# A second path through a transformer block: where its code lies, and how the kernel ends

## The chip, the core and the metric

The kernel runs on one core of a Trainium2 chip. The metric is the device time of one execution in microseconds (us), reported as the median of several runs. Each of the core's engines (TensorE or PE, VectorE or DVE, ScalarE or ACT, GpSimd or POOL, SyncE or SP) has its own stream of instructions; semaphores order them against each other. A branch is taken by each engine for itself.

## The reference

One block of a transformer in pre-norm form, sequence 2048, width 640, in bf16: attention with 32 query heads of 20 columns that share one key and one value head, then a gated feed-forward layer of width 1536.

```python
def _A_ref(x, wq, wk, wv, wo):
    q = heads(x @ wq); k = x @ wk; v = x @ wv
    scores = jnp.einsum("bhqd,bkd->bhqk", q, k) * (Dh ** -0.5)
    p = _softmax(scores, axis=-1)
    ...
    return o @ wo

def _B_ref(x, w_gate, w_up, w_down):
    h = _gelu(x @ w_gate) * (x @ w_up)
    return h @ w_down

h  = x + _A_ref(_layernorm(x), ...)
h2 = h + _B_ref(_layernorm(h), ...)
```

## The kernel before

**Two paths.** The main path computes the softmax without subtracting row maxima: it exponentiates the scores as they are, sums them with the values (a column of ones in `v_ext` gives the sum), and divides. That is right as long as the sums are neither too small nor too large. So the kernel checks the reciprocals of all sums (`rL`) against two bounds, brings the outcome into one integer (`flag`), and every engine loads it into a register (`good`). If all is well, each engine branches to the block `all_done`; otherwise it falls into the block `with_maximum`, which computes everything again with row maxima. With the inputs of the reference the second path is not run, but its code lies between the branch and `all_done` in each engine's stream.

**The planner.** Every piece of work is a task (`sc.add`) with its engine, an estimated duration, dependencies, a priority and the buffers it takes and gives back. `_Sched.schedule` runs them in simulation and writes down one order for each engine (`order`), `resolve` works out the semaphore waits, `emit` writes the instructions. `HOT` is a large negative priority (first come), `hold` lets a task reserve its engine for a moment. Nothing is reordered at run time.

**The work.** Sixteen tiles of 128 rows. The scores of a tile go through PSUM in groups of two or three banks to ScalarE's exponential (L978, tile `pbuf`); some go to VectorE instead (L932, L943, tile `dbuf`). TensorE multiplies the result with `v_ext`. Between them TensorE does the projections and the feed-forward matmuls of earlier tiles (L534), whose results VectorE adds to the rows in `xh` (L1276). SP issues all transfers and DMA transposes after the start.

**The last tile** (`last_tile`) has no other attention work to hide behind, and is laid out for a short chain: transposed sums and their reciprocal (L1111, L1113), normalised output (L1118), transposes and copy (L1139, L1142), the output projection into two PSUM banks (L1308, tasks `wa`, `wb`), statistics of the layer norm (L1322) and copies to `xh` by ACT (L1324, task `bx`), normalisation (L1328 to L1334, the power on POOL, L1331), transposes (L1348) and copies by ACT and DVE (L1355, tasks `bte`), the residual into the accumulators (L1301, task `again`), gate and up matmuls (L1372), GELU (L1399), product (L1404), down matmuls (L1381), eviction of the two halves (L1415, tasks `fin`) and their output (L1417). ACT's table for the GELU is loaded right behind the last exponential (L1339).

**The end of the main path.** `raise_flag` is called after `last_tile`. The checks of all sums but the last pass come early; those of the last pass are held back behind the layer norm of the last tile (`state["last_nm"]`): three small DVE operations (L1157, L1159, L1161), a product (L1168), a matmul with a constant that spreads the outcome over the partitions (L1171, task `okm`), a conversion to an integer (L1173), the register load on each engine (L1178) and, right behind it, a branch hint on each engine (L1179): an instruction that names the target of a later branch ahead of time. `run` wraps each path in a block (`nc.Block`, L1498), which ends with a barrier of all engines. Then comes the branch (L1527), and in `all_done` SP waits until all outputs have landed (the wait's record has line L1520).

Of the kernel before, what the change touches and what calls it, by code (L numbers as in the profile page):

```python
# [45 lines left out]
class _Sched:  # L46
# [363 lines left out]
    def emit(self, eng_name, eng, sems):  # L410
        for t in self.order[eng_name]:
            for s, v in self.waits.get(t, ()):
                eng.wait_ge(sems[s], v)
            ins = t.fn(eng)
            if t.sem is not None:
                ins.then_inc(sems[t.sem], 16 if t.dma is not None else 1)


def bass_sequential_preLN__grouped_kv_mqa__glu_gated_geglu__prompt_kernel(
# [308 lines left out]
    q_ready, q_evicted, q_slot = {}, {}, {}  # L728
    all_qk = {}
# [21 lines left out]
    def q_dma(t, tk, g0=0):  # L751
        tr = sc.add("sp", lambda e: e.dma_start_transpose(
            qT[:, q_slot[t].index, g0:NG, :], q_tok[:, tk.index, 4 * g0:H, :].rearrange("p a b -> p (a b)")),
# [14 lines left out]
    def q_first(tk):  # L768
# [23 lines left out]
        for j, eng in ((0, "act"), (1, "dve")):  # L792
# [12 lines left out]
            def ev(e, j=j, eng=eng, view=view):  # L805
                o = qT[:, q_slot[0].index, 2 * j:2 * j + 2, :]
# [68 lines left out]
    def qk_mm(e, bk, item):  # L875
        t, h, kt, hl = item
        r = slice(32 * hl, 32 * hl + 32)
        return e.matmul(bk.rearrange("p (g n) -> p g n", g=4), kT4[r, kt * P:(kt + 1) * P],  # L878
                        qT[r, q_slot[t].index, 4 * h:4 * h + 4, :], start=True, stop=True, tile_position=(32 * hl, 0))
# [285 lines left out]
    def raise_flag():  # L1165
        early = check_sums(0, 2 * NT - 1, 0, 0.45)
        late = check_sums(2 * NT - 1, 2 * NT, 1, 0.14, [state["last_nm"]])
        c = sc.add("dve", lambda e: e.tensor_tensor(okay_b[:], okay_all[:, 0:1], okay_all[:, 1:2], ALU.mult), 0.2,  # L1168
                   [early, late], prio=HOT + 2, name="okb")
        ax, bk = aux()  # L1170
        m = sc.add("pe", lambda e: e.matmul(bk()[:, 0:1], halves[:, 0:P], okay_b[:], start=True, stop=True), 0.1,  # L1171
                   [c, t_halves], prio=HOT / 4, acq=[ax], name="okm")
        f = sc.add("dve", lambda e: e.tensor_scalar(flag[:], bk()[:, 0:1], 2.0, None, ALU.mult), 0.2, [m], prio=HOT / 4,  # L1173
                   rel=[ax], name="flag")

        for eng in sc.ENGINES:
            def fn(e, eng=eng):
                ins = e.reg_load(good[e.engine], flag[0:1, 0:1])  # L1178
                hints[e.engine] = e.mark_branch_hint_location()  # L1179
                return ins  # L1180
            sc.add(eng, fn, 0.6, [f], prio=1e6, after=late_on.get(eng, []), name=f"good_{eng}")

    late_on = {}
# [99 lines left out]
    def last_tile(t, ont):  # L1283
# [37 lines left out]
        for j, c0, c1 in halves_:  # L1321
# [17 lines left out]
        tab = sc.add("act", lambda e: e.activation(warm[:], warm[:], ACT.Gelu_apprx_tanh), 2.7, state["exps"], prio=1e7,  # L1339
                     name="gelu_table")  # L1340
        lnT = []
# [17 lines left out]
        late_on["act"], late_on["dve"] = lnT[:1], lnT[1:]  # L1359
# [52 lines left out]
        downs(2)  # L1412
        for j, c0, c1 in halves_:
            fin = add("dve" if j else "act", lambda e, j=j, c0=c0, c1=c1: (
                e.tensor_copy(xh[:, t, c0:c1], acc(j)) if j else e.activation(xh[:, t, c0:c1], acc(j), ACT.Copy)), 0.45,  # L1415
                [dn[j], nm], rel=[a_sl], name=f"fin{j}_{t}")
            outs.append(sc.add("sp", lambda e, c0=c0, c1=c1: e.dma_start(out_view[:, t, c0:c1], xh[:, t, c0:c1]), 2.0,  # L1417
                               [fin], prio=nprio(), dma="d_out", name=f"out{j}_{t}"))

# [57 lines left out]
    raise_flag()  # L1477
# [11 lines left out]
    sem_cms = []  # L1489

    def run(plan, wait_out):
# [6 lines left out]
        with nc.Block() as block:  # L1498

            @block.sync  # L1500
            def _(e):
                wait_out(e)
                plan.emit("sp", e, sems)

            @block.scalar
            def _(e):
                plan.emit("act", e, sems)

            @block.tensor
            def _(e):  # L1510
                plan.emit("pe", e, sems)

            @block.vector
            def _(e):
                plan.emit("dve", e, sems)

            @block.gpsimd
            def _(e):
                plan.emit("pool", e, sems)
        return lambda e: e.wait_ge(sems["d_out"], plan.totals["d_out"])  # L1520

    out_done = run(sc, lambda e: None)


    for e in nc.engines.values():
        if e.engine in hints:
            e.br_eq(good, P, on_true="all_done", on_false="with_maximum").branch_hint(hints[e.engine])  # L1527
    with nc.body("with_maximum"):
        sc = _Sched()
        SA_pool, PV_pool, AUX_pool = _Pool(1), _Pool(1), _Pool(2)  # L1530
        LN_pool, XN_pool, ON_pool, ONT_pool, HH_pool, G_pool = (_Pool(4), _Pool(NXB), _Pool(1), _Pool(2), _Pool(2),
                                                                _Pool(2))
        OTK_pool, QTK_pool, QT_pool = _Pool(2), _Pool(2), _Pool(1)
        PR_pool, PT_pool, MX_pool = _Pool(NPB), _Pool(2), _Pool(2)
        t_half = t_ident = dma_wg = dma_wu = dma_wd = None
        z_q, tail, q_evicted, state["qk"] = [], [None, "d_oT"], {}, None
        dma_wq = [None, None]
        wo_ready, outs = [], []
        last_in = None

        def head(t, g, hl, q_done, q_sl, heads):

            r = slice(32 * hl, 32 * hl + 32)
            s_sl, p_sl, t_sl, m_sl = SA_pool.slot(), PR_pool.slot(), PT_pool.slot(), MX_pool.slot()
# [95 lines left out]
```

## Time and profile before

| | |
|---|---|
| time, median of 3 runs | 761.51 us (759.73 to 764.65) |
| profiled execution: time | 761.73 us |
| profiled execution: span, first to last instruction | 760.0 us |
| PE busy | 720.2 us (95%) |
| ACT busy | 728.3 us (96%) |
| DVE busy | 675.8 us (89%) |
| POOL busy | 190.3 us (25%) |
| mean granted TensorE clock | 0.990 |

The span counts from the first to the last instruction record of any engine, branches and semaphore waits included, while "busy" leaves those out. The execution's time is 1.7 us longer than its span. In the rows of the profile, "PEld" is TensorE's weight load, "SPq", "PEldq" and the like are an engine's queue instructions (loads of registers, branches, waits), "L1178" is line 1178 of the kernel before. A row of a line's records reads: engine, operation, count, shortest/median/longest duration in ns, start of the first and the last. The window rows read: window, its length, busy time and count of PE, PEld, DVE, ACT and POOL, the granted clock, the share of the DMA engines, GB/s.

### The profile page before, as it was taken

How to read it: one execution, taken by the hardware profiler on the slowest of the kernel's cores; microseconds unless marked ns; L12 is line 12 of the kernel's file. 1: busy time of each engine (PE TensorE's matmuls, PEld its weight loads, DVE VectorE, ACT ScalarE, POOL GpSimd, SP SyncE). 2: the span in 40 equal slices, each digit the busy share in tenths (PEclk: the TensorE clock that was granted, in tenths of full speed). 3: DMA queues.
4: the chain of work that ended last, by engine and by line, in shares of the span. 5: the costliest groups of instructions: out<-in, count | busy, mean ns of one | idle time of the engine just before them, and what ended most of it. 6: DMA issues, size and time to landing. Idle time of an engine off the chain costs nothing.

```text
span 760.0 us, 23793 instructions
## 1 busy us (share of the span) xinstructions
PE 720.2 (95%) x10601; PEld 262.3 (35%) x10601; DVE 675.8 (89%) x1271; ACT 728.3 (96%) x701; POOL 190.3 (25%) x257
## 2 busy tenths in 40 slices
PE   7889889999999999999999999999999999999996
PEld 3332223333333333333333333333333332323335
DVE  8679999997998899999998988998999999898872
ACT  6899999999999999999999999999999999999981
POOL 6310001151335134103304133140321012251500
PEclk9699999999999999999999999999999999999999
DMA  6893011020111102120100202012021200110020
GB/s 172 135 343 73 1 26 17 2 45 19 24 31 41 33 2 46 20 45 19 31 16 19 45 20 46 19 16 45 5 46 31 41 11 10 40 22 20 14 52 22
DMA packets 80623, 31.68 MB, mean 42 GB/s; under 512 B 71552, under 2 KB 79232, under 8 KB 80512
## 3 DMA queue, kind: packets, MB, share of 16 engines
q1 hardware_dynamic: 79200, 30.03, 18.4%
q8 instruction: 84, 1.38, 0.8%
q10 hardware_dynamic: 1312, 0.05, 0.1%
q14 instruction: 27, 0.22, 0.1%
HBM read 10.21 MB, written 2.62 MB: 17 GB/s over the span
## 4 chain that ended last, share of the span: by engine, by line
ACT 61%; PE 28%; DVE 7%; DMA 2%; POOL 1%; issue 0%
ACT pbuf L978 60%; PE ps L534 10%; PE ps L878 9%; PE ps L1092 7%; DVE dbuf L932 2%; ACT g_z L1257 1%; DMA xnT<-xn_tmp 1%; PE ps L1372 1%; DVE dbuf L943 1%; DMA onT<-oN 1%; POOL g_z L1217 0%; DVE g_us L1251 0%; PE ps L1381 0%; DVE xn_tmp L649 0%; DVE stats L626 0%
## 5 line engine op out<-in xcount | busy, mean ns | idle before, releaser
L978 ACT ACTIVATE pbuf<-ps 128x1024 bf16<-128x1024 f32 (+1 forms) x661 | 700.8, 1226 | 6.1 <-PE ps L878 5.4
L932 DVE TENSOR_SCALAR dbuf<-ps 128x512 int16<-128x512 f32 x520 | 341.5, 681 | 35.9 <-PE ps L878 33.2
L878 PE MATMUL ps<-qT,kT 32*128 32x512 bf16 x2048 | 289.0, 387 | 17.1 <-ACT pbuf L978 12.0
L943 DVE TENSOR_SCALAR dbuf<-dbuf 128x2048 int16<-128x2048 int16 x260 | 172.8, 690 | 0.7
L878 PEld LDWEIGHTS ps<-qT,kT 32*128 32x128 bf16 x2048 | 76.2, 91 | 255.4 <-ACT pbuf L978 191.5
L1092 PE MATMUL ps<-pbuf,v_ext 128*32 128x512 bf16 (+3 forms) x2032 | 146.1, 334 | 1.7 <-ACT pbuf L978 1.5
L1092 PE MATMUL ps<-dbuf,v_w 128*32 128x512 bf16 x1560 | 133.9, 382 | 4.3 <-DVE dbuf L932 1.7
L1245 POOL TENSOR_TENSOR g_z<-g_gs 128x512 bf16<-128x512 bf16 x45 | 48.7, 1082 | 131.2 <-DVE g_gs L1243 131.2
L1092 PEld LDWEIGHTS ps<-pbuf,v_ext 128*32 128x32 bf16 x2032 | 44.4, 94 | 71.3 <-issue 51.1
L534 PE MATMUL ps<-wg_sb,xnT 128*32 128x512 bf16 x900 | 67.9, 383 | 0.7 <-DVE dbuf L932 0.2
L534 PE MATMUL ps<-wd_sb,hhT 128*32 128x320 bf16 x1440 | 67.6, 301 | 0.5 <-DMA hhT<-g_us 0.2
L534 PE MATMUL ps<-wu_sb,xnT 128*32 128x512 bf16 x900 | 67.3, 382 | 0.5
L1118 POOL TENSOR_TENSOR oN<-oT,rL 128x320 bf16<-128x320 f32 x30 | 22.2, 739 | 160.0 <-DVE rL L1113 159.7
L1092 PEld LDWEIGHTS ps<-dbuf,v_w 128*32 128x32 bf16 x1560 | 38.5, 95 | 40.7 <-DVE dbuf L943 12.5
L632 POOL CAST lnvb<-mv 128x1 bf16<-128x1 f32 x31 | 7.3, 236 | 171.5 <-DVE mv L630 170.8
L1217 POOL TENSOR_TENSOR g_z<-g_z,g_gs 128x512 bf16<-128x512 bf16 x36 | 41.1, 1168 | 30.5 <-DVE g_z L1254 30.5
L1217 POOL TENSOR_TENSOR g_us<-g_z,g_us 128x512 bf16<-128x512 bf16 x36 | 40.6, 1155 | 24.7 <-DVE g_z L1260 24.7
L534 PEld LDWEIGHTS ps<-wd_sb,hhT 128*32 128x32 bf16 x1440 | 31.9, 96 | 26.6 <-issue 15.8
L1251 DVE SCALAR_TENSOR_TENSOR g_us<-ps,g_gs 128x512 bf16<-128x512 f32 x45 | 30.6, 681 | 4.9 <-PE ps L534 4.7
L534 PE MATMUL ps<-wq_sb,xnT 128*32 128x320 bf16 (+1 forms) x660 | 31.7, 298 | 1.1 <-DVE xnT L682 0.4
L1243 DVE CAST g_gs<-ps 128x512 bf16<-128x512 f32 x45 | 30.4, 676 | 1.7 <-PE ps L534 1.5
L534 PE MATMUL ps<-wo_sb,onT 128*32 128x320 bf16 x600 | 30.5, 302 | 1.3 <-DVE dbuf L932 0.8
(98 smaller groups left out, 363.5 us busy)
## 6 DMA issues: line engine op xcount, KB each, us to landing
out_dram<-xh SPq DMA_DIRECT2D x15, 160.0 KB, 1.8
wg_sb<-in_B_w_gate_dram SPq DMA_DIRECT2D x1, 1920.0 KB, 10.6
wu_sb<-in_B_w_up_dram SPq DMA_DIRECT2D x1, 1920.0 KB, 15.0
wd_sb<-in_B_w_down_dram SPq DMA_DIRECT2D x1, 1920.0 KB, 19.7
xh<-in_A_x_dram SPq DMA_DIRECT2D x2, 640.0 KB, 7.1
xh<-in_A_x_dram SPq DMA_DIRECT2D x3, 320.0 KB, 3.8
wq_sb<-in_A_wq_dram SPq DMA_DIRECT2D x2, 400.0 KB, 4.9
wo_sb<-in_A_wo_dram SPq DMA_DIRECT2D x1, 800.0 KB, 4.9
```

The lines of the kernel that those rows point to most:

```text
L534: ins = e.matmul(out[r, :], lhs[:, r], rhs, start=start, stop=stop, tile_position=(0, 32 * b))
L878: return e.matmul(bk.rearrange("p (g n) -> p g n", g=4), kT4[r, kt * P:(kt + 1) * P], qT[r, q_slot[t].index, 4 * h:4 * h + 4, :], start=Tr ...
L932: quad["bits"].append(sc.add("dve", lambda e: e.tensor_scalar(part(seg, w=slice(512 * item[0], 512 * item[0] + 512)), bk(), D_BIAS, 0.0, A ...
L943: dep = [sc.add("dve", lambda e, j=j, s=s: e.tensor_scalar(part(s), part(seg), D_SHIFT[j], None, ALU.add), 0.602, bits, prio=0.55 * HOT + ...
L978: exps.append(sc.add("act", lambda e, w0=w0, w1=w1, to=to: e.activation(pbuf[:, to:to + w1 - w0], ps[:, w0:w1], ACT.Exp, scale=EXP_SCALE), ...
L1092: ins = e.matmul(ps[32 * b:32 * b + 32, PVB * 512 + a:PVB * 512 + a + n].rearrange("p (a n) -> p a n", n=32), x[2], span.rearrange("p (a n ...
L1118: onorm[(t, h)] = c = sc.add(by, lambda e: e.tensor_tensor(oN[:, otk.index, h * (D // 2):(h + 1) * (D // 2)].rearrange("p (g l d) -> p l g ...
L1217: return [sc.add("pool", lambda e, c=slice(512 * j, 512 * j + 512): e.tensor_tensor(out[:, k.index, c], a[:, k.index, c], b[:, k.index, c] ...
L1243: ge = sc.add("dve", lambda e, col=col, bk=bk: e.tensor_copy(g_gs[:, gsl.index, col], bk()), d_ps(512), [gm], prio=EVAC + pr, rel=[ax], na ...
L1245: sqt = sc.add("pool", lambda e, col=col: e.tensor_tensor(g_z[:, gsl.index, col], g_gs[:, gsl.index, col], g_gs[:, gsl.index, col], ALU.mult),
L1251: uts.append(sc.add("dve", lambda e, col=col, bk=bk: e.scalar_tensor_tensor(g_us[:, gsl.index, col], bk(), 0.5, g_gs[:, gsl.index, col], A ...
L1257: th = sc.add("act", lambda e: e.activation(g_z[:, gsl.index, :], g_z[:, gsl.index, :], ACT.Tanh, scale=GELU_C), d_act(1536), zt, prio=-5. ...
```

## The change

It moves code, and with it the jumps over it, and it moves the checks.

- **Place of the second path's code.** For SP, POOL and ACT it now lies in the middle of the main path, in a block `with_maximum_1`; they jump over it there without condition (SP and POOL where the planner's order has their widest gap, ACT behind the last exponential). In the order that results, SP jumps behind the transpose of the queries that follows the first tile's output transpose, POOL behind its last product `g_z` of the feed-forward layer. At the end these three fall through to `all_done` when the flag is good and go back to `with_maximum_1` when it is not. For PE and DVE the second path (`with_maximum_2`) stays at the end, and they branch over it.
- **No block, no barrier.** The orders are emitted straight into the program; the barrier between the two paths is replaced by waits at the head of the second path.
- **Checks.** The checks of the last pass no longer wait for the layer norm. In DVE's order two stand before the copy of L1142, the minimum and the product behind it, the integer flag behind L1330. The matmul `okm` stands behind L1308 on PE and uses the bank of the attention sums. The register loads stand at the end of each stream on SP, ACT and PE (behind its last down matmuls), on DVE before the three products of L1404.
- **Hint.** Only PE has one, right behind L1308 (task `wb`), ahead of 36 of the matmuls of L534 that lay before L1301; four of the 40 now lie behind it.
- **Last eviction.** Both halves of the last output are evicted by ACT.
- **GELU table.** Its load stands behind ACT's copies of L1324.

```diff
 def raise_flag():
     early = check_sums(0, 2 * NT - 1, 0, 0.45)
-    late = check_sums(2 * NT - 1, 2 * NT, 1, 0.14, [state["last_nm"]])
+    late = check_sums(2 * NT - 1, 2 * NT, 1, 0.14)
...
-    ax, bk = aux()
+    ax, bk = pvb()
...
-            ins = e.reg_load(good[e.engine], flag[0:1, 0:1])
-            hints[e.engine] = e.mark_branch_hint_location()
...
+def flag_loads(f):
+    late_on.update(act=[ends[-1]], pe=[ends[0]], sp=outs[-1:])
+    for eng in sc.ENGINES:
+        sc.add(eng, lambda e: e.reg_load(good[e.engine], flag[0:1, 0:1]), 0.55, [f],
+               prio=1e6 if eng != "dve" else HOT, after=late_on.get(eng, []), name=f"good_{eng}")
...
 # last_tile
-    tab = sc.add("act", lambda e: e.activation(warm[:], warm[:], ACT.Gelu_apprx_tanh), 2.7, state["exps"], prio=1e7,
+    tab = sc.add("act", lambda e: e.activation(warm[:], warm[:], ACT.Gelu_apprx_tanh), 1.5, ev, prio=HOT,
                  name="gelu_table")
+    def hint(e):
+        hints[e.engine] = e.mark_branch_hint_location()
+    early.append(sc.add("pe", hint, 0.05, [wb[-1]], prio=HOT, name="hint"))
...
+    flag_up = raise_flag()
...
-        fin = add("dve" if j else "act", lambda e, j=j, c0=c0, c1=c1: (
-            e.tensor_copy(xh[:, t, c0:c1], acc(j)) if j else e.activation(xh[:, t, c0:c1], acc(j), ACT.Copy)), 0.45,
+        fin = add("act", lambda e, j=j, c0=c0, c1=c1: e.activation(xh[:, t, c0:c1], acc(j), ACT.Copy), 0.45,
...
 # after the schedule of the main path
+over = {"sp": widest(first.order["sp"]), "pool": widest(first.order["pool"]),
+        "act": 1 + max(i for i, x in enumerate(o) if x in state["exps"])}
+for e, n in over.items():
+    first.emit(e, handle[e], first_sems, 0, n)
+first_bb = nc.cur_bb
+nc.br("with_the_rest")
...
+with nc.body("with_maximum_1", valid_engines=OVER):
+    recompute(over)
+    nc.sync.wait_ge(again_sems["d_out"], again.totals["d_out"])
+    nc.br("all_done", engines=OVER)
+nc.switch_bb("with_the_rest")
+for e in handle:
+    first.emit(e, handle[e], first_sems, over.get(e, 0))
+branch(over, "with_maximum_2", "with_maximum_1")
+branch(("pe", "dve"), "all_done", "with_maximum_2")
+with nc.body("with_maximum_2"):
+    recompute(("pe", "dve"))
     nc.br("all_done")
-nc.switch_bb("all_done")
-out_done(nc.sync)
+nc.switch_bb("all_done", parent=first_bb)
+nc.sync.wait_ge(first_sems["d_out"], first.totals["d_out"])
```

More of the change, by code (lines that the diff above doesn't have):

```diff
@@ L1496, in run @@
             sem_cms.append(cm)
[L1498 to L1519, printed above, removed]
@@ new lines, in semaphores, with widest @@
+        return sems
+    def widest(o):
+        return max(range(1, len(o)), key=lambda i: o[i].start - o[i - 1].end)
+    first = sc
+    first_sems = semaphores(first)
+    o = first.order["act"]
+    over = {"sp": widest(first.order["sp"]), "pool": widest(first.order["pool"]),
+            "act": 1 + max(i for i, x in enumerate(o) if x in state["exps"])}
+    OVER = [handle[e].engine for e in over]
+    for e, n in over.items():
+        first.emit(e, handle[e], first_sems, 0, n)
+    first_bb = nc.cur_bb
```

194 lines of the change are left out of this document (102 added, 92 removed).

## The prediction, made before the result was known

> **What bounds the kernel now.** I read the page first, then the end of the chain of waits, then the records of the lines at the end, because the change leaves the order of work before the last tile alone.
>
> ```profile
> span 760.0 us, 23793 instructions
> PE 720.2 (95%) x10601; PEld 262.3 (35%) x10601; DVE 675.8 (89%) x1271; ACT 728.3 (96%) x701; POOL 190.3 (25%) x257
> ACT 61%; PE 28%; DVE 7%; DMA 2%; POOL 1%; issue 0%
> ```
>
> ScalarE's exponentials carry 61% of the chain and TensorE fills most of the rest. Comparing the instruction order of both kernels engine by engine, every instruction up to the last exponential stands where it stood, so 735 us of the span can change only through the jumps discussed below. The end of the chain of waits is where to look:
>
> ```profile
> 753.56 0.05 PE ps L1171
> 753.61 0.48 DVE xh L1415
> ```
>
> The columns are start, length, engine, tile and line. The last eviction of the output ends at 754.09 and DVE writes the flag just behind it, yet the span ends at 760.0. The records of the queues' own instructions (line, queue, count, duration in ns, first and last start) fill in these 5.9 us:
>
> ```profile
> L1178 SPq TENSOR_LOAD <-flag x1: 514/514/514, 754.5 to 754.5; - x1
> ...
> L1179 PEldq BRANCH_PREFETCH_HINT  x1: 45/45/45, 754.8 to 754.8; - x1
> L1179 SPq BRANCH_PREFETCH_HINT  x1: 51/51/51, 755.1 to 755.1; - x1
> ...
> L1527 SPq COMPARE_BRANCH  x1: 73/73/73, 755.4 to 755.4; - x1
> L1527 PEldq COMPARE_BRANCH  x1: 4531/4531/4531, 755.5 to 755.5; - x1
> ...
> L1520 SPq EVENT_SEMAPHORE  x1: 17/17/17, 758.8 to 758.8; - x1
> ```
>
> The flag is loaded (0.5 us), the hint is given, a barrier joins the engines, and all branch over the code with row maxima at 755.4 to 755.5. SP's next instruction, the wait for the outputs, runs at 758.8, 3.4 after its branch; PE's branch itself lasts 4.53 and ends the span at 760.0. The outputs aren't what is waited for, as the landing time shows:
>
> ```profile
> 753.05 0.44 ACT L1415 ACTIVATE xh<-ps 128x320 bf16<-128x320 f32 x1 [2.15 <-PE ps L1381]
> 753.60 0.49 DVE L1415 CAST xh<-ps 128x320 bf16<-128x320 f32 x1 [1.48 <-PE ps L1171]
> L1417 SPq DMA_DIRECT2D out_dram<-xh x2: 332/332/332, 753.5 to 754.1; - x2
> DMA to landing us min/median/max: 1.6/1.6/1.6
> ```
>
> The last half of the output is issued at 754.1 and lands 1.6 later, at 755.7. What is waited for is code; the DMA queues in the window 756 to 757 show it (packets, MB):
>
> ```profile
> q14 instruction: 4, 0.03, 11.4%
> q8 instruction: 1, 0.02, 9.8%
> ```
>
> Five fetches, one for each engine. So the engines jump over long code, their targets aren't at hand, and fetching costs 3.4 (SP) to 4.5 us (PE) from the branch, or, from the hint, 3.7 (755.1 to 758.8) to 5.2 (754.8 to 760.0). That stretch is **the bound of the end**; the time outside the span is 761.73 - 760.0 = 1.73.
>
> **The change, part by part.** *The skipped code of SP, POOL and ACT* goes to the middle of their streams, so each takes one jump there, and their last branch goes on to the next instruction. A jump without a hint costs 3.4 to 5.2 by the rows above. Who covers it:
>
> ```profile
> 73.15 1.23 SPq L752 DMA_TRANSPOSE qT<-q_tok  x1
> 108.68 1.20 SPq L1125 DMA_TRANSPOSE onT<-oN  x1
> ...
> 740.49 0.55 POOL L1331 TENSOR_TENSOR lnden<-lnve,halfc 128x1 bf16<-128x1 bf16 x1 [18.63 <-DVE lnve L1330]
> ...
> 734.24 1.13 ACT L978 ACTIVATE pbuf<-ps 128x1024 bf16<-128x1024 f32 x1
> 735.39 1.28 ACT L1339 ACT_TABLE_LOAD   x1
> 736.68 0.20 ACT L1339 ACTIVATE warm<-warm 128x1 f32<-128x1 f32 x1
> 739.41 0.85 ACT L1324 ACTIVATE xh<-ps 128x320 bf16<-128x320 f32 x2 [2.52 <-DVE stats L1322]
> 742.47 0.49 ACT L1355 ACTIVATE xnT<-ps 128x384 bf16<-128x384 bf16 x1 [2.22 <-PE ps L1348]
> ...
> 740.65 0.45 PE L1301 MATMUL ps<-xh,ident 128*128 128x320 bf16 x2
> ```
>
> SP jumps behind the transfer at 73.15 and has nothing until 108.68: over 30 us of cover, and no queue is moved past another. POOL jumps in its 18.63 us of idleness before L1331. ACT is the close one: it jumps behind the last exponential. If the queue goes on when that one starts (734.24), the target is there at 737.6 to 739.4, for work at 739.41. If it goes on only when the exponential ends (735.37), 738.8 to 740.6: up to 1.2 late, of which 0.4 is free, because the matmuls on ACT's copy ("again", L1301) run at 740.65 and the copy ends at 740.26; so 0 to 0.8. I take 0: the fetches were on q14, whose SP row gives 3.4. The table load that moves behind that copy takes 1.28 + 0.20 from 740.26, to 741.75; the next ACT work is at 742.47, so 0.7 us cover it. If ACT were 1.2 late, that cover would be gone and 0.5 would show.
>
> *The last checks* leave the end:
>
> ```profile
> 737.84 0.36 DVE L1142 COPY onT<-ps 128x384 bf16<-128x384 bf16 x1 [0.43 <-PE ps L1139]
> 738.88 0.91 DVE L1322 BATCH_NORM_STATS2 stats<-ps 128x6 f32<-128x320 f32 x2 [0.68 <-PE ps L1308]
> 740.33 0.48 DVE L1276 TENSOR_TENSOR xh<-xh,ps 128x320 bf16<-128x320 bf16 x1
> 741.08 0.16 DVE L1333 RECIPROCAL lnr<-lnden 128x1 f32<-128x1 bf16 x1 [0.28 <-POOL lnden L1331]
> 742.62 0.17 DVE L1159 SCALAR_TENSOR_TENSOR wk<-rL,wk 128x16 bf16<-128x16 f32 x1
> 742.82 0.17 DVE L1161 TENSOR_REDUCE okay_all<-wk 128x1 f32<-128x16 bf16 x1
> 743.29 0.15 DVE L1168 TENSOR_TENSOR okay_b<-okay_all 128x1 bf16<-128x1 f32 x1
> ```
>
> Two checks (0.17 each) go into the idle 0.43 before the copy of L1142, the minimum and the product (0.17 + 0.15) into the 0.68 before the statistics, the flag (0.15) ahead of the sum at 740.33, which leaves 0.13 of the 0.28 before the reciprocal. All fit: 0, at most 0.1 each for the first and the last, at least 0. DVE's flag load (0.5) stands where DVE waits over 2 us for TensorE. The matmul that spreads the flag comes into TensorE's work:
>
> ```profile
> 753.26 0.10 PEld L1171 LDWEIGHTS ps<-okay_b,halves 128*128 128x128 bf16 x1
> 753.40 0.17 PE L1171 MATMUL ps<-okay_b,halves 128*128 128x1 bf16 x1
> ...
> 742.21 0.49 DVE L1276 TENSOR_TENSOR xh<-xh,ps 128x320 bf16<-128x320 bf16 x1 [0.40 <-PE ps L534]
> ...
> 742.76 0.28 PE L1348 MATMUL ps<-ident,xn_tmp 128*128 128x128 bf16 x2 [0.32 <-DVE xh L1276]
> ```
>
> It goes between the matmuls of L1308 and those of L534, where TensorE works without a gap; DVE's sum of L1276 waits for the last of L534, and the transposes of L1348 wait for that sum. So it is on the path, at a price between 0 and 0.10 + 0.17 = 0.27; I take 0.13, the distance of its load to its matmul. Four of the matmuls of L534 pass behind L1301, which changes no total. At the old place it held up nothing, since the copy waits for the downs only.
>
> *The last eviction* goes from DVE (0.49) to ACT (0.44). ACT ends its first at 753.49, before the second may start at 753.60, so nothing queues: -0.05.
>
> *The end.* The second eviction ends at 753.60 + 0.13 + 0.44 = 754.17; its DMA starts 0.03 later, lands 1.6 after that: **755.80**. SP's issue (0.33) and load (0.51) lie inside, and there is no barrier and no jump before its wait. PE ends its matmuls at 753.69, loads for 0.51 as SP did, branches at 754.2. Its hint now stands behind L1308, at 739.2, 15 us ahead; then the branch should cost what SP's own record shows, 0.1. DVE branches without a hint behind its last product:
>
> ```profile
> L1404 DVE TENSOR_TENSOR hhT<-ps,g_gs x3: 691/691/692, 745.9 to 751.4; 128x512 bf16<-128x512 f32 x3
> ```
>
> From 751.6, with 3.4 to 5.2, DVE is through at 755.0 to 756.8; SP's 3.4 is the nearest (same queue), so 755.0, hidden by the DMA; at 5.2 it would end 1.0 later than SP. Sum: 760.0 - 755.8 = 4.2 less; 761.73 - 4.2 = **757.5 us**. The profiled execution is 0.2 above the median 761.51, within the runs' spread.
>
> The Trainium skill speaks against this ("Runtime: NRT & Kernel Launch", section Instruction fetch mechanics): a taken branch whose target is outside a window of two pages has to fetch it before going on. The trace agrees, with 3.4 to 4.5 us. By that rule the three jumps in the middle pay too, under the cover above, and a page fetched 15 us early would be gone: the first rival.
>
> **The rivals.** *The hint is lost.* How far TensorE runs between hint and branch:
>
> ```profile
> 739.20:753.60 14.40, 13.66 (x221) 11.07 (x220) 5.37 (x18) 3.57 (x7) 0.55 (x1) 1.00 0.04 13
> q8 instruction: 84, 1.38, 0.8%
> ```
>
> The 84 fetches of q8 over 10601 matmuls and as many loads are one per 252 instructions; 441 instructions after the hint mean one or two further fetches, which could push the target out. For it: no hint in this trace stands that far ahead. Against it: the hint is an order of its own for a target far off. Then PE branches at 754.2 and pays 4.5 to 5.2: 758.7 to 759.4, or 760.4 to 761.1 us.
>
> *Another fetch shows at the end.* In before, q14 fetches four more blocks while PE still waits; if DVE must cross into a next block after its jump, 3.4 follow 755.0: 758.4, or 760.1 us. Against it: those four came after 758 with nothing seen to wait for them.
>
> *Slower: the hint takes the place of the block TensorE needs next.* Place: the first of the crossings between 739.2 and 753.6, on the path. Price 4.5 there, and with the target lost too, 4.5 at the branch: 754.2 + 4.5 + 4.5 = 763.2, or 764.9 us; two crossings, 769.4. It decides as soon as such a wait exceeds 4.2, the whole gain. Against it: the early fetches of before never stopped PE (issue 0% of the chain).
>
> *The change doesn't do what it says*: the jumps themselves show, ACT's most (0.8 + 0.5): 758.8. That lies inside the range.
>
> **How the numbers follow.** Forecast 0.70, hint lost 0.14, another fetch 0.08, slower 0.08. The forecast's own range is 755.5 to 759.5 (the runs of before lie 2 below to 3 above the profiled one; the costs bounded above add up to 2). Down to 755.3 and up to 761.4 the first two rivals are in; left out are the slower case and tails, under 0.2. A difference of 1%, 7.6 us, is about what a measurement of this kernel tells from none. Faster than that would need more than all that stands after 754.2, outside time included (7.6): 0.03. Slower needs two lost crossings: 0.03. Within 1%: 0.94.
>
> **What would show it.** Right: PE's branch at some 0.1 us near 754.2, its fetch near 740 to 742, SP's wait for the outputs as the last record near 755.8, ACT's copy of L1324 still near 739.4, no barrier. Wrong: PE's branch over 3 us (hint lost); a gap in TensorE's matmuls between 740 and 753 with a fetch of q8 at its end (slower); ACT's copy later than 739.8; a DVE branch that lasts past 755.8.

## The result, and the profile after

The changed kernel takes **759.14 us** (median of 9 runs, 757.11 to 762.09) against 762.02 of the kernel before (9 runs, 759.73 to 764.65): ratio 0.9956, 95% interval 0.9936 to 0.9975. A second comparison gave 757.66 (11 runs) against 761.81 (27 runs), and the same ratio, 0.9956 (0.9929 to 0.9983). So it is faster by 0.25% to 0.64%: 1.9 to 4.9 us, less than the 1% that the forecast called no change.

The profiled execution of after is the slowest of its nine runs, 762.09 with a span of 760.8, and beside the 760.0 of before it seems to have gained nothing. Its page:

```profile
span 760.8 us, 23781 instructions
PE 723.5 (95%) x10601; PEld 262.8 (35%) x10601; DVE 675.4 (89%) x1270; ACT 729.2 (96%) x702; POOL 189.8 (25%) x257
```

The engines do the same work as before, and PE is busy for 3.3 us longer, at a granted clock of 0.987 against 0.990. So the end must be read by itself. The records of the lines that answer to those shown of before (line, queue, count, duration in ns, first and last start):

```profile
L1344 PEldq BRANCH_PREFETCH_HINT  x1: 45/45/45, 741.9 to 741.9; - x1
...
L1608 DVEq COMPARE_BRANCH  x1: 72/72/72, 755.4 to 755.4; - x1
L1608 PEldq COMPARE_BRANCH  x1: 402/402/402, 756.7 to 756.7; - x1
...
L1608 SPq COMPARE_BRANCH  x1: 53/53/53, 759.0 to 759.0; - x1
...
L1421 ACT ACTIVATE xh<-ps x2: 437/437/437, 757.1 to 757.6; 128x320 bf16<-128x320 f32 x2
...
L1423 SPq DMA_DIRECT2D out_dram<-xh x2: 332/332/332, 757.5 to 758.1; - x2
DMA to landing us min/median/max: 2.0/2.3/2.7
...
L1625 SPq EVENT_SEMAPHORE  x1: 17/17/17, 760.8 to 760.8; - x1
```

There is no barrier left, PE's branch with the hint 15 us ahead takes 0.402 instead of 4.531, SP falls through, and the last record is SP's wait for the outputs. I call the start of the last eviction F (757.60; 753.60 before) and count from it. The second half of the output is issued at F + 0.46 and takes 2.7 to land, which gives F + 3.16, where SP's wait stands: the end now waits for data, not for code. The execution's time is F + 4.49 after, F + 8.13 before. **The end is 3.64 us shorter**, though the halves of the output take 2.0 and 2.7 to land where both took 1.6.

What took the gain back in this one execution lies ahead of F. The rows below are windows (window, length, busy time and count of PE, PEld, DVE, ACT, POOL, granted clock, DMA share, GB/s). The first goes from the end of the last exponential to the first gate matmul in after, the second is a part of it. Then come the same stretch in a second profile of the changed kernel and in before:

```profile
737.97:747.43 9.46, 8.69 (x128) 4.35 (x128) 5.60 (x19) 2.82 (x6) 0.55 (x1) 0.82 0.04 12
738.80:742.20 3.40, 3.40 (x36) 1.27 (x33) 2.00 (x8) 0.00 (x0) 0.00 (x0) 0.50 0.03 7
```

```profile
734.44:742.50 8.06, 7.24 (x127) 3.99 (x127) 5.59 (x19) 2.82 (x6) 0.55 (x1) 1.00 0.04 14
```

```profile
735.37:743.43 8.06, 7.24 (x127) 3.91 (x127) 5.43 (x18) 2.82 (x5) 0.55 (x1) 1.00 0.03 12
```

At full clock the stretch lasts 8.06 us in both kernels. In the profiled execution of after it lasts 9.46, because the throttle granted half the clock for 3.4 us in it. Such stretches of half clock fall in some executions and not in others, in either order of the work: the first experiment below, which keeps the order of before, has one there too and takes 9.43. So they aren't an effect of the change. The single times scatter by some 6 us, the longer ones mostly at a lower granted clock (756.71 at 0.998, 762.75 at 0.984, both of the changed kernel). Each experiment below is therefore read by its tail, the time from F to the end. Where a kernel was profiled once, its tail is that of one execution.

### The profile page after: what moved, and what is told of

Its sections match the earlier page's. It is cut to its first block, busy times and chain, and to the rows that moved or that the text cites. A ratio compares the mean times of both kernels' runs of the same rounds, so it can differ in the third digit from the quotient of the medians.

```text
span 760.8 us, 23781 instructions
## 1 busy us (share of the span) xinstructions
PE 723.5 (95%) x10601; PEld 262.8 (35%) x10601; DVE 675.4 (89%) x1270; ACT 729.2 (96%) x702; POOL 189.8 (25%) x257
## 3 DMA queue, kind: packets, MB, share of 16 engines
q8 instruction: 84, 1.38, 0.8%
## 4 chain that ended last, share of the span: by engine, by line
ACT 53%; PE 32%; DVE 7%; DMA 5%; POOL 1%; issue 0%
ACT pbuf L979 51%; PE ps L534 12%; PE ps L879 10%; PE ps L1093 8%; DVE dbuf L933 3%; DMA qT<-q_tok 2%; ACT g_z L1258 1%; DVE dbuf L944 1%; DMA xnT<-xn_tmp 1%; PE ps L1378 1%; DMA hhT<-g_us 1%; DVE g_us L1252 1%; DMA onT<-oN 1%; DVE xn_tmp L649 0%; POOL g_z L1218 0%
## 5 line engine op out<-in xcount | busy, mean ns | idle before, releaser
L534 PE MATMUL ps<-wd_sb,hhT 128*32 128x320 bf16 x1440 | 68.5, 305 | 0.8 <-DMA hhT<-g_us 0.5
L534 PE MATMUL ps<-wg_sb,xnT 128*32 128x512 bf16 x900 | 67.9, 383 | 0.7 <-DVE dbuf L933 0.2
L534 PE MATMUL ps<-wu_sb,xnT 128*32 128x512 bf16 x900 | 67.3, 382 | 0.4
L534 PEld LDWEIGHTS ps<-wd_sb,hhT 128*32 128x32 bf16 x1440 | 32.1, 96 | 27.5 <-issue 15.9
L534 PE MATMUL ps<-wq_sb,xnT 128*32 128x320 bf16 (+1 forms) x660 | 32.2, 301 | 1.1 <-DVE xnT L682 0.4
L534 PE MATMUL ps<-wo_sb,onT 128*32 128x320 bf16 x600 | 30.5, 302 | 1.5 <-DVE dbuf L933 0.8
```

What stands on the lines that cost most here:

```text
L534: ins = e.matmul(out[r, :], lhs[:, r], rhs, start=start, stop=stop, tile_position=(0, 32 * b))
```

## The experiments

The table counts from F. "Landing" is the time from issue to landing of the second half of the output; SP's wait ends with it wherever no code is fetched for SP itself (all rows but "before" and "early hints only"). "Fetches" are the code fetches that start between F and F + 2 (q8 is PE's queue with blocks of 0.02 MB, q14 that of the others with 0.01 MB).

| kernel | SP's wait | landing | fetches | time | PE's branch |
|---|---|---|---|---|---|
| before | +5.23 | 1.6 | none | +8.13 | 4.531 |
| after | +3.16 | 2.7 | q8 +0.86, q14 +1.31 | +4.49 | 0.402 |
| after, second profile | +2.86 | 2.4 | q8 +0.27, q14 +1.33 | +4.30 | 0.402 |
| early hints only | +5.63 | 1.6 | none | +7.12 | 0.402 |
| no hint | +3.26 | 2.8 | q8 +0.18, q14 +1.56 | +4.80 | 3.907 |
| all in the middle | +2.06 | 1.6 | none | +3.50 | 0.093 |
| DVE evicts | +2.95 | 2.4 | q8 +0.27, q14 +1.05 | +4.57 | 0.402 |
| table early | +3.11 | 2.6 | q8 +0.27, q14 +1.41 | +4.43 | 0.402 |
| PE in the middle | +2.90 | 2.4 | q14 +1.34 | +4.78 | 0.093 |
| late checks | +2.07 | 1.6 | q8 +1.92, q14 +1.98 | +5.23 | 0.402 |
| hint later | +3.35 | 2.9 | q8 +0.53, q14 +1.51 | +4.68 | 0.491 |
| both hints | +2.07 | 1.6 | none | +3.39 | 0.093 |
| DVE hint too | +2.80 | 2.3 | q8 +0.51 | +4.23 | 0.402 |

**Is it the place of the code, or would early hints do?** This is the kernel before with its hints moved far ahead on all engines; the code of the second path and the barrier stay in place:

```diff
-                ins = e.reg_load(good[e.engine], flag[0:1, 0:1])
-                hints[e.engine] = e.mark_branch_hint_location()
-                return ins
+                return e.reg_load(good[e.engine], flag[0:1, 0:1])
...
+        for eng, at in (("pe", wb[-1]), ("act", state["exps"][-1]), ("dve", nm), ("pool", pw), ("sp", onT_done[(t, 0)])):
+            sc.add(eng, hint, 0.05, [], prio=HOT, after=[at], name=f"hint_{eng}")
```

> The kernel before with one edit: each engine's branch hint stands 12 to 18 us ahead (PE behind L1308, ACT behind the last exponential, DVE behind the normalisation, POOL behind its last power, SP behind its first transpose of the last tile) instead of right before the barrier. The code with row maxima, the barrier, the late checks and the eviction by DVE stay. All times from F, the start of the second eviction (before: SP's wait for the outputs at F+5.2, PE's branch ends at F+6.4, the time is F+8.1; changed kernel: F+3.2 and F+4.5). Theory (fetching the branch targets bounds the end, and a hint far ahead takes that away wherever the code lies): PE's branch takes about 0.4 us, SP's wait comes at F+2.0 to F+2.4, the time is F+3.7 to F+4.3, some 4 us less than before. Rival 1 (the place of the code matters: a hint that far ahead is lost on the engines with small fetches, only code put elsewhere helps): SP's wait still at about F+5.2, PE's branch short or not, time F+6.5 to F+8.1.

Its records, and the code fetches in the window 757.5 to 758.6:

```profile
L1337 SPq BRANCH_PREFETCH_HINT  x1: 51/51/51, 715.8 to 715.8; - x1
...
L1337 PEldq BRANCH_PREFETCH_HINT  x1: 45/45/45, 739.4 to 739.4; - x1
...
L1530 SPq COMPARE_BRANCH  x1: 73/73/73, 756.8 to 756.8; - x1
...
L1530 PEldq COMPARE_BRANCH  x1: 402/402/402, 756.9 to 756.9; - x1
...
L1523 SPq EVENT_SEMAPHORE  x1: 17/17/17, 760.8 to 760.8; - x1
```

```profile
q14 instruction: 4, 0.03, 10.3%
q8 instruction: 1, 0.02, 7.0%
```

PE's hint, 17.5 us old, held (0.402). SP's, 41 us old, did not: its wait stands 3.9 us after its branch (3.4 in before). Four fetches of q14 start about 1 us after the branches, one for each engine on that queue, so by this the hints of ACT, POOL and DVE, 14 to 23 us old, were lost as well. That is the rival's outcome. By the tail 1.0 us is gained (F + 7.12 against F + 8.13); the medians, 761.91 us against 761.51, ratio 1.0013 (0.9983 to 1.0042), show no gain. Both PE and SP had to fetch at the end, and curing PE alone leaves SP. An early hint did not cure SP; in the changed kernel, where SP has no code to jump over at the end, its wait comes 2.5 to 2.8 us earlier than here. What the barrier costs by itself no run shows; SP's branch stands at F + 1.81 with it and at F + 1.42 without it in after.

**What is the remaining hint worth?** The changed kernel without it:

```diff
-        early.append(sc.add("pe", hint, 0.05, [wb[-1]], prio=HOT, name="hint"))
```

> The changed kernel without PE's hint; its order is otherwise the same. Theory: PE's branch, at F-0.85 as in the changed kernel, takes 3.4 to 4.5 us instead of 0.40 and ends at F+2.6 to F+3.7; the time is F+4.5 to F+5.5, against F+4.5 with the hint, so the hint is worth 0 to 1 us here, because the wait for the outputs (F+3.2) hides most of it. Rival (the branch was short because there is no barrier and no fetch is needed, not because of the hint): the branch stays at about 0.4 us.

Its records:

```profile
L1607 PEldq COMPARE_BRANCH  x1: 3907/3907/3907, 755.2 to 755.2; - x1
...
L1422 SPq DMA_DIRECT2D out_dram<-xh x2: 332/930/1529, 756.0 to 756.5; - x2
...
DMA to landing us min/median/max: 2.8/2.8/2.9
```

Without the hint PE pays 3.9, but from F - 0.86 to F + 3.05, which ends before SP's wait at F + 3.26. The time is F + 4.80: in this kernel the hint is worth 0.3 to 0.5, not the 2.9 to 3.6 that the prediction's rival ("the hint is lost") gave it. The Trainium skill ("Runtime: NRT & Kernel Launch", section Instruction fetch mechanics) says that a taken branch out of the window of two pages waits for a fetch; the 3.907 here agrees, and the 0.402 of after shows that a hint gets round it.

**Does PE's and DVE's code belong in the middle too?** All five engines jump once in the middle, PE and DVE with a hint 10 us ahead:

```diff
+    o = first.order["dve"]
+    over["dve"] = [x.name for x in o].index(f"t1_{NT - 1}_1")
...
+        if e in ("pe", "dve"):
+            o = first.order[e]
+            m = max(i for i in range(n) if o[i].start < o[n].start - HINT_AHEAD)
...
-    branch(("pe", "dve"), "all_done", "with_maximum_2")
...
```

> The changed kernel with PE's and DVE's code of the second path in the middle too: each jumps over it where it waits for the last exponential, with a hint 10 us ahead of that jump; at the end all five engines go on to the next instruction. So nothing is fetched at the end. Theory (the second half of the output landed 2.7 us after its issue in the changed kernel, 1.6 before, because fetches of code ran beside it: PE's 16 KB at F+0.9 to F+1.8 and an 8 KB one at F+1.3 to F+2.1): it lands after 1.6 us, SP's wait comes at F+2.1, the time is F+3.4 to F+3.6, 1 us less than the changed kernel's F+4.5. Rival (the landing is longer since the two halves follow each other closer, 0.54 against 0.60 us, or by chance): 2.3 to 2.7 us again and F+4.5. The two jumps in the middle cost nothing if the hints hold (PE's idle time there is over 1 us); if not, 3 us between the last exponential and the transposes of its sums.

A record, the timeline of DVE, and the window from the last exponential's end to the first gate matmul:

```profile
L1534 DVEq COMPARE_BRANCH  x1: 80/80/80, 733.4 to 733.4; - x1
```

```profile
737.87 0.72 DVE L1112 STREAM_TRANSPOSE oT<-ps 128x512 f32<-128x512 f32 x1 [4.04 <-issue]
```

```profile
735.41:747.00 11.59, 8.89 (x127) 4.52 (x128) 5.78 (x19) 2.85 (x6) 0.55 (x1) 0.85 0.05 11
```

The transpose as it stands in the second profile of after:

```profile
734.95 0.72 DVE L1112 STREAM_TRANSPOSE oT<-ps 128x512 f32<-128x512 f32 x1 [2.09 <-PE ps L1093]
```

The DMA issues at the end of this run:

```profile
out_dram<-xh SPq DMA_DIRECT2D x2, 80.0 KB, 1.6
```

The end is the shortest so far (F + 3.50, landing 1.6 again). The two halves are still issued 0.54 apart, so it is not their distance that makes them land late, as the rival had it. But DVE's hint was lost in the middle: the transpose of the sums, which is on the chain, waits 4.04 instead of 2.09, for nothing but "issue". That is 2.0 of the 3.5 by which the window exceeds 8.06; the rest goes with a stretch of half clock (0.85 in the row). The time is 760.37 us, ratio 0.998 (0.9961 to 0.9999): what the end gained went, in part, into a jump at a place where nothing covers it. No cost of PE's jump in the middle was seen.

**Which of the two fetches is it, and does a hint help DVE?** Two kernels, run beside the changed one: PE's code in the middle and DVE's at the end ("PE in the middle"), and the same with a second hint for DVE's branch, 160 instructions ahead ("both hints"):

```diff
+    over["pe"] = max((i for i in range(1, len(o)) if o[i].start > last_exp - 1.0 and o[i].name != f"res_{NT - 1}" and o[i].start < last_exp + 2.0),
+                     key=lambda i: o[i].start - o[i - 1].end)
...
+        if e == "dve":
+            a = len(first.order[e]) - DVE_AHEAD
+            first.emit(e, handle[e], first_sems, 0, a)
+            hints[handle[e].engine] = handle[e].mark_branch_hint_location()
...
```

> The changed kernel with PE's part of the second path in the middle too, jumped over where PE waits for the last exponential, hint 10 us ahead; DVE's part stays at the end as in the changed kernel. F is the start of the second eviction, X the start of the last exponential. Theory (the output lands late in the changed kernel because code is fetched beside it, by PE 16 KB and by DVE 8 KB): without PE's fetch the last packet of the output ends at F+1.7 to F+2.2 instead of F+2.6, SP's wait comes at F+2.1 to F+2.6, the time is F+3.5 to F+4.0 against F+4.5; X to F is unchanged at full clock. Rival (DVE's fetch alone does it): packets until F+2.6 again and F+4.5.

> The same as the kernel with PE's part in the middle, and DVE gets a hint for its branch at the end, 160 instructions ahead of the end of its stream, so that DVE fetches a next block between hint and branch. Theory (a hint is carried out when the engine next fetches a block; so far only PE's hints, with a block's fetch behind them, held, while hints without one were lost: SP's 40 us ahead, DVE's 10 us ahead of its jump in the middle): DVE's hint holds, no fetch of the target at F-1.1, the block after it comes at about F-1.4 instead of F+1.3 to F+1.6, so no fetch runs beside the output: SP's wait at F+2.1, time F+3.5. Rival (hints work on PE alone): the target's fetch at F-1.1 and the next at F+1.3 to F+1.6 as in the changed kernel, time as in the kernel without this hint.

> The changed kernel once more, beside the others on one chip. Theory: from F to the end 4.4 to 4.8 us, against 8.1 before; from the end of the last exponential to the first gate matmul 8.06 at full clock as before, 9.4 to 9.5 where TensorE is granted half its clock for 3.4 us in that stretch, which happens by chance in both kernels. So 3.3 to 3.7 us less than before in the median, ratio 0.995 to 0.996. Rival (the change makes the half clock in that stretch more frequent): 9.4 to 9.5 here too, and a median gain of 2.0 to 2.5 us.

The code fetch in the window 755.4 to 757.9 and the landing of the output in the first, then the records of the second:

```profile
q14 instruction: 1, 0.01, 1.7%
...
DMA to landing us min/median/max: 1.6/2.0/2.4
```

```profile
L1636 DVEq BRANCH_PREFETCH_HINT  x1: 51/51/51, 641.5 to 641.5; - x1
...
L1622 DVEq COMPARE_BRANCH  x1: 84/84/84, 750.6 to 750.6; - x1
L1622 PEldq COMPARE_BRANCH  x1: 93/93/93, 751.9 to 751.9; - x1
...
DMA to landing us min/median/max: 1.6/1.6/1.6
...
L1644 SPq EVENT_SEMAPHORE  x1: 17/17/17, 754.8 to 754.8; - x1
```

With DVE's fetch alone beside the output the first half lands in 1.6, the second in 2.4, and SP's wait stands at F + 2.90, which lies between the two profiles of the changed kernel (F + 2.86 and F + 3.16); the theory's F + 2.1 to F + 2.6 and its time of F + 3.5 to F + 4.0 were missed (F + 4.78). One more fetch of q14 starts at F + 4.65 there; whose it is, and whether the end waits for it, is open. With neither fetch both halves land in 1.6, and SP's wait stands at F + 2.07; so DVE's hint held, against the rival that hints work on PE alone. Medians: 759.97 for the first (ratio 0.9959, 0.9934 to 0.9984), **757.01** with both hints (ratio 0.9927, 0.9899 to 0.9955), 757.66 for the changed kernel (0.9956). The changed kernel's tail, F + 4.30, is a little under the 4.4 to 4.8 expected of it, and its stretch ahead of the gates is 8.06, against the rival. The version with both hints is faster than the kernel before, and by its tail 0.9 to 1.1 us better than the changed one; the intervals of the ratios overlap, so the runs don't show that last step by themselves.

**Does PE's fetch alone delay the output?** The changed kernel with DVE's early hint; PE's code stays at the end:

```diff
+    DVE_AHEAD = 160
...
+        if e == "dve":
+            a = len(first.order[e]) - DVE_AHEAD
+            first.emit(e, handle[e], first_sems, 0, a)
+            hints[handle[e].engine] = handle[e].mark_branch_hint_location()
...
```

> The changed kernel with a second hint: VectorE's branch at the end gets one 160 instructions ahead, as in the version with both; TensorE's code stays at the end with its own hint. So of the two engines whose next block was fetched beside the output, TensorE is left. F is the start of the second eviction. Theory (each such fetch beside the output delays its landing by itself): VectorE's target is fetched at the hint and its next block before F; TensorE's next block is still fetched at F+0.2 to F+0.9; the output's last packet ends at F+2.0 to F+2.6 and SP's wait stands at F+2.4 to F+3.0 (changed kernel F+2.5 to F+2.6 and F+2.9 to F+3.2; only VectorE's fetch left: F+2.4 and F+2.9; none left: F+1.7 and F+2.1). Rival (VectorE's fetch alone delays the output, since it shares a queue with it): F+1.7 and F+2.1, as with both moved.

The code fetch in its window 758.1 to 760.5, and the landing:

```profile
q8 instruction: 1, 0.02, 2.4%
...
DMA to landing us min/median/max: 1.9/2.1/2.3
```

With PE's fetch alone the halves land in 1.9 and 2.3, and the last packet ends at F + 2.26 (F + 1.69 with none): either queue's fetch delays the output by itself, as the theory had it. But one fetch delays the second half nearly as much as two do (2.3 and 2.4 against 2.4 to 2.9), so both had to go.

**Does it matter which engine evicts?** The second half of the last output is evicted by DVE again (ACT then loads the flag behind its own half):

```diff
...
-        fin = add("act", lambda e, j=j, c0=c0, c1=c1: e.activation(xh[:, t, c0:c1], acc(j), ACT.Copy), 0.45,
+        fin = add("dve" if j else "act", lambda e, j=j, c0=c0, c1=c1: (
+            e.tensor_copy(xh[:, t, c0:c1], acc(j)) if j else e.activation(xh[:, t, c0:c1], acc(j), ACT.Copy)), 0.45,
```

> The changed kernel, but the second half of the last output is evicted by VectorE again, as in the kernel before; so VectorE's flag load stays ahead of its products, but its branch (without a hint) can only come behind that eviction. F is the start of the second eviction. Theory (what moving it to ScalarE bought is that VectorE's jump begins 2 us earlier): VectorE branches at F+0.5 to F+0.6 instead of F-2.2, its target is fetched at about F+1.5 instead of F-1.1, its next block at about F+4; VectorE is through at F+4 to F+5, after SP's wait for the outputs (F+2.5 to F+3.2), and the time is F+5.3 to F+6.3 (the changed kernel: F+4.3 to F+4.5). Rival (which engine evicts does not matter, as my sum had it: -0.05): time at F+4.3 to F+4.6.

Its records:

```profile
L1609 DVEq COMPARE_BRANCH  x1: 72/72/72, 753.1 to 753.1; - x1
...
L1626 SPq EVENT_SEMAPHORE  x1: 17/17/17, 756.0 to 756.0; - x1
```

The branch moved by 2.2 us, but stands at F + 0.01, beside the eviction and not behind it as the theory had it: the queue went on while VectorE still worked. Fetches of q14 start at F + 1.05 (the target) and F + 3.65 (a next block), and the time is F + 4.57: the rival's number. The moved eviction is worth 0.3 at most.

**Does it matter when the flag is known?** The checks are held back to the end again, and with them the flag loads, DVE's too; the rest is as changed:

```diff
-        late = check_sums(2 * NT - 1, 2 * NT, 1, 0.14)
+        late = check_sums(2 * NT - 1, 2 * NT, 1, 0.14, [state["last_nm"]])
...
-        flag_up = raise_flag()
...
-        flag_loads(flag_up)
+        flag_loads(raise_flag())
```

> The changed kernel, but the checks of the last pass are held back behind the layer norm of the last tile again, the matmul that spreads the flag stands behind the last down matmuls, and every engine loads the flag at the end; code, hint and evictions stay as changed. Theory (early checks matter, because the jumps that are left at the end wait for the flag): the flag is written at about F+0.3 to F+0.5, the loads end at about F+1, VectorE branches (without a hint) at about F+1 instead of F-2.2 and is through at F+4 to F+5, TensorE's branch with its early hint takes 0.4 from F+1; the time is F+5.3 to F+6.3. Rival (the checks cost nothing at the end once the code has moved, since SP's wait for the outputs hides them): F+4.3 to F+4.6. By both the stretch from the end of the last exponential to the first gate matmul stays at 8.06 us at full clock, as the matmul that spreads the flag cost nothing measurable there.

Its records, then the code fetches in 755.3 to 756.0 and in 758.0 to 758.6:

```profile
L1607 DVEq COMPARE_BRANCH  x1: 72/72/72, 754.3 to 754.3; - x1
...
DMA to landing us min/median/max: 1.6/1.6/1.6
...
L1624 SPq EVENT_SEMAPHORE  x1: 17/17/17, 755.5 to 755.5; - x1
```

```profile
q8 instruction: 1, 0.02, 11.8%
q14 instruction: 1, 0.01, 3.9%
...
q14 instruction: 1, 0.01, 3.2%
```

The most telling run. The fetches come too late to disturb the output, which lands in 1.6, and SP's wait stands at F + 2.07; yet the time is F + 5.23, 3.1 us after the last record. DVE branches without a hint at F + 0.81, and q14 fetches its target at F + 1.98 and a second block at F + 4.63. The execution ends behind that, 0.6 after the start of the last fetch; that it waits for this fetch is the likely reading, not a measured wait, since the span holds no record there. So early checks are worth 0.7 to 0.9 us: they let DVE's jump begin 3 us earlier, which costs landing time and still gains. The time lay just under the theory's 5.3 to 6.3 and far from the rival's. The stretch ahead of the gates was 8.06, as both had it.

**What does ACT's jump cost?** The table load is back behind the last exponential, so it is the first instruction behind ACT's jump:

```diff
-        tab = sc.add("act", lambda e: e.activation(warm[:], warm[:], ACT.Gelu_apprx_tanh), 1.5, ev, prio=HOT,
+        tab = sc.add("act", lambda e: e.activation(warm[:], warm[:], ACT.Gelu_apprx_tanh), 2.7, state["exps"], prio=1e7,
```

> The changed kernel with ACT's load of the GELU table back behind the last exponential, where it is the first instruction after ACT's jump and so shows when the jump is over. Before, it started 1.15 us after the start of the last exponential (734.24 to 735.39), at once when that had ended. Theory (a jump without a hint costs 3.4 us or more from where the queue takes it, and the queue takes it when the last exponential starts): the table load starts 3.4 to 4 us after the last exponential's start. If the queue takes the jump only when the exponential ends: 4.5 to 5.2. Rival (an unconditional jump is cheap): 1.2 to 1.5. In no case should the time from the last exponential to F move by more than 0.3, since ACT's next work stands 4 us behind the end of the exponential.

ACT's jump and its timeline:

```profile
L1520 ACTq COMPARE_BRANCH  x1: 38/38/38, 737.3 to 737.3; - x1
```

```profile
733.08 5.60 ACT L979 ACTIVATE pbuf<-ps 128x1536 bf16<-128x1536 f32 x5
740.11 1.28 ACT L1340 ACT_TABLE_LOAD   x1 [1.43 <-issue]
...
742.72 0.84 ACT L1325 ACTIVATE xh<-ps 128x320 bf16<-128x320 f32 x2 [1.11 <-DVE stats L1323]
```

The first instruction behind the jump starts 1.43 after the exponentials' end at 738.68, 2.56 after the start of the last one (737.55): this bounds the jump at about 2.6 (2.8 from the branch's own record, at 737.3), most of it covered by that exponential. It lies between the theory's 3.4 to 4 and the rival's 1.2 to 1.5; both were missed. The copy comes 4.04 after the exponential's end, as in before (739.41 - 735.37). Time F + 4.43: the place of the table load makes no difference.

**Does the hint act only when PE next fetches?** It was moved to 5.7 us ahead of F, past PE's last fetch before the branch:

```diff
-        early.append(sc.add("pe", hint, 0.05, [wb[-1]], prio=HOT, name="hint"))
...
+            if i == 2:
+                pe_last = sc.add("pe", hint, 0.05, [dn[1]], prio=HOT, name="hint")
```

> The changed kernel with PE's hint not at F-14.3 but behind the first down matmuls, at about F-4.7, that is behind the last fetch of a block (F-8.2) and 3.8 us ahead of the branch (F-0.86). Theory (a hint is carried out only with the engine's next fetch of a block): the hint is lost, the branch takes 3.9 us as without a hint, its fetch is at F+0.2. Rival (a hint needs only time): a fetch at F-3.7, the branch 0.1 to 0.5 us.

Records of the hint and the branch, and the window 750 to 752:

```profile
L1344 PEldq BRANCH_PREFETCH_HINT  x1: 45/45/45, 749.5 to 749.5; - x1
...
L1609 PEldq COMPARE_BRANCH  x1: 491/491/491, 754.5 to 754.5; - x1
```

```profile
q8 instruction: 1, 0.02, 3.0%
```

A fetch starts 1.3 after the hint and the branch is short, so on PE a hint can fetch by itself; the theory that it needs another fetch fell. (The hint also changed the planner's order: the stage ahead of F is 0.96 longer.)

## Why the prediction was right, and where its sum was off

The forecast was 757.5 us, a gain of 4.2; the tails of two profiles give 3.64 and 3.83, the two medians 2.9 and 4.2. The first median, 759.14, lies inside the forecast's range, 0.4 below its upper bound; the second, 757.66, lies 0.2 from the forecast itself, and that closeness is luck in part, since the terms below miss by more. The mechanism was right; the terms:

- **The bound of the end** (fetching branch targets): right. Early hints alone, which leave SP's fetch, gain 1.0 of the 8.1 behind F.
- **SP and POOL jump under cover**: no cost of theirs was seen; the last tile's two stages (8.06 to the gates, 10.17 from there to F) are those of before at equal clock.
- **ACT's jump**, 3.4 priced, 0 taken: the price is 2.6 to 2.8, and 0 was right. The table load behind the copies was covered, as said.
- **Checks in DVE's gaps**: right, 0. What they buy was not in the sum as a term of its own: 0.7 to 0.9 us.
- **The matmul that spreads the flag**, +0.13: wrong, 0.00. The stretch is 8.06 with and without it. The step that failed is "where TensorE works without a gap". In the second profile of after:

```profile
738.02 0.10 PEld L1172 LDWEIGHTS ps<-okay_b,halves 128*128 128x128 bf16 x1
738.15 0.17 PE L1172 MATMUL ps<-okay_b,halves 128*128 128x1 bf16 x1
738.25 1.07 PEld L534 LDWEIGHTS ps<-wd_sb,hhT 128*32 128x32 bf16 x36
```

and the same place in before:

```profile
739.17 1.21 PEld L534 LDWEIGHTS ps<-wd_sb,hhT 128*32 128x32 bf16 x40 [0.26 <-issue]
```

In before TensorE's loads stand still for 0.26 ahead of those of L534, for no wait but "issue", and these start 3.80 after the last exponential's end; in after they start 3.81 after it, with no such idle time. The matmul sits in that 0.26, a gap of the loads that the prediction's rows did not show.

The other terms:

- **Last eviction on ACT**, -0.05: not to be told from zero; DVE's branch 2 us earlier, of which the prediction said only that it would be hidden, is worth at most 0.3.
- **PE's branch**, at 754.2 (F + 0.47) for 0.1: it stands at F - 0.86, since PE's queue loads the flag while the last matmuls still run, and took 0.40; 0.09 is what a branch costs that goes on to the next instruction. That is also why a lost hint is cheap: the 3.9 from there is nearly hidden. "Its fetch near 740 to 742" was not seen as one of its own: q8 starts fetches at 740.95, ahead of the hint, and at 749.38, and without the hint there are two such as well. Whether the second was already the target's is open.
- **DVE's unhinted jump, hidden**: right for the time, wrong on its fetches. The prediction weighed them only as a wait of DVE itself ("another fetch shows at the end"); in after they show as a longer transfer.
- **Landing 1.6**: the mis-sized term. The second half took 2.4 and 2.7 in the two profiles of after, and SP's wait came at F + 2.86 and F + 3.16 where the sum has 755.80 for an F of 753.73, or F + 2.07. The three kernels with no fetch beside the output have that 2.06 to 2.07 exactly.
- **1.73 outside the span**: from SP's wait to the end it is 1.33 and 1.44 in the two profiles of after, which gave back 0.3 to 0.4 of the 0.8 to 1.1. In before, fetches still run at F + 5.4 to F + 8.2, behind SP's wait; in after none does. That this makes the difference is likely, not shown.

The errors cancel in part: +0.8 to +1.1 for the landing, -0.3 to -0.4 outside and -0.13 for the matmul leave 0.4 to 0.6 less gain than forecast. Of the rivals, the lost hint was refuted (0.402), and even a lost hint would not have cost what it was priced at. No gap of PE ahead of F bore out the slower one, and no cost of the jumps the last one (8.06 and 10.17, as in before).

## What to carry to other kernels

A branch to code that isn't at hand cost 2.6 to 4.5 us here on ACT, SP and PE, so put code that is not run where its engine idles anyway, engine by engine, and look at which engine's fetch ends last: curing one of two gained little here, both times that it was tried (early hints, and the fetches beside the output). At the end of a kernel, keep code fetches away from the last output transfer, or start them before it. Compare tails from a common point when clock stretches of several us scatter the totals.

## What the runs showed of the hardware that I had not expected

- A code fetch of 8 or 16 KB beside an output of 160 KB in 288 packets makes its second half land 0.7 to 1.3 us later: 1.6 with none (five profiles), 2.3 and 2.4 with one, 2.4 to 2.9 with two. PE's fetch delays both halves, DVE's at F + 1.34 only the second. How so few bytes do it is open.
- Where PE's fetch starts before SP's second output issue, that issue takes 1.13, 1.17, 1.38 and 1.53 us (fetch at F + 0.27, F + 0.27, F + 0.27, F + 0.18); where it starts behind the issue at F + 0.46, 0.33 (F + 0.51, F + 0.53, F + 0.86). The order is the same in all seven; the cause wasn't tried.
- A hint right ahead of its branch didn't help: before's PE paid 4.531 with one 0.7 us ahead, the changed kernel's 3.907 without any. On PE, hints 5 to 17 us ahead held. On the engines with blocks of 8 KB, SP's at 41 us, those of ACT, POOL and DVE at 14 to 23 us (early hints only) and DVE's 9 us ahead in the middle were lost. DVE's 109 us ahead of its last branch held, as far as one fetch less behind the branch tells. What decides this is open.
- The execution ended 3.1 us after its last record where a fetch of code started 2.6 after that record (late checks), against 1.3 to 1.9 otherwise.
